# Attention stage: TensorE's work in runs of one block size, in a new order per unit

## Chip, cores and metric

The kernel runs on one core of a Trainium2 chip. The metric is the device time of one execution in microseconds; the time before is the median of three runs.

## Reference

Three layers follow each other. The change touches the first alone.

```python
def _attn_ref(q, k, v):                      # q, k, v: (4, 8, 576, 64)
    ...
    q_d, k_d, v_d = means of 4 neighbouring rows            # 144 rows
    out_up = np.repeat(sm_attn(q_d, k_d, v_d), 4, axis=2)   # full softmax attention of the pooled rows
    mask = np.abs(pos[:, None] - pos[None, :]) < 4
    scores = np.where(mask, scale * q @ k.T, -1e9)          # a band of 7 keys per query
    out_local = softmax(scores) @ v
    return out_up + out_local
...
x = attn_out.transpose(0, 2, 1, 3).reshape(B * S, H * D)    # (2304, 512)
x = _moe_ref(x, phi, w1, w2)     # soft mixture: logits = x @ phi, 8 experts with 4 slots each
return _moe2_ref(x, w_gate, w_noise, noise, w1, w2)         # top-2 mixture of 8 experts
```

The setup multiplies q, k and w_noise by 8 after drawing them.

## The kernel before

The attention runs over 16 units, a unit being one batch and two heads, whose two 64-wide heads fill the 128 partitions. A step loop `for p in range(-1, NU - 1)` (L586) goes through the list `SEQ` (L19) once per step and issues each named step for the unit `p - off`, where `off` stands in the table `BL` (L550); the last units are issued from the list `TSEQ` (L21). Each engine works through its own instructions in the order of these lists, so `SEQ` sets the order on every engine and on SP's queue of transfers. No scheduler changes it.

The steps of a unit u, in the order of their data:

- `ld` (L181, two steps ahead): keys and queries of the unit are loaded into `ld`, four transfers on SP's queue in rows of 64 floats; two buffers. `lV` (L197, one step ahead): four transfers for the values, two buffers, so unit u's can start when unit u - 2 has used its own.
- `A0`, `A1` (`a_pe`, L225, one step ahead): six transposes each, of keys and of queries. `a00` to `a111` (L235) evict them to `K` and `Q`. `KD` (L253) sums four neighbouring keys on GpSimd; `DQ0` and `DQ1` (L242) do so for the queries of one head each, `DQ0` on GpSimd in two additions, `DQ1` on VectorE in one reduce.
- `S` (`b_s`, L283): the band's scores in PSUM, a bf16 matmul that writes the mask (L285), then 20 matmuls of 35 columns (L289). `SD` (L294): pooled scores (L300). `M`, `EL`, `EX`, `SU`, `P0`, `P1` are the band's softmax, the last two on GpSimd (L333); `MD`, `DX`, `RD`, `DM` are the pooled one, of which `DM` (L362), the division by the sum, runs on GpSimd in place.
- one step later: `CP` and `CD` (L370, L380) transpose the two attention matrices; `EP00` to `EP11`, `ED0`, `ED1` evict them to `PT` and `PdT`. `VD` (L261) pools the values by matmuls, `V0`, `V1` evict them to `Vd`. `DP` (L405) and `DD` (L417) multiply by the values, `DD` with 128 and then 16 rows. `x0`, `x1`, `XA` evict and add.
- two steps later: `EP` (L437) transposes the unit's output, `X0`, `X1` keep it, `LG` (L459) computes the slot logits with four matmuls of 128 columns into 32 partitions each and a fifth into all 128, `LA` adds them up. Every fourth step also has the slots' softmax and sums (`SE`, `SS`, `ST`, `SU_`, `SK`).

All transposes and `LG` write to a ring of four PSUM buffers (`tp`, L176), so each waits until the one four before it has been evicted. `W` (L602) issues one megabyte of the soft mixture's weights per step (two in the first), of which eight matrices of two megabytes are loaded during the attention, three more when the attention's memory is free (`R2`), and the other five as buffers are released by the soft mixture's matmuls (L795, L817). `cp` (L217) puts an eviction on VectorE if its name is in `ON_V`, else on ScalarE.

## Time and profile before

| | us |
|---|---|
| median of three runs | 496.54 (495.12 to 497.39) |
| the profiled execution | 494.55 |
| its span, first to last instruction | 492.7 |
| TensorE busy | 470.2 (95%) |
| VectorE, ScalarE, GpSimd busy | 277.4, 263.4, 199.2 |

The attention's first scores start at 7 us and those of the last unit at 141 us; the soft mixture runs to about 200 us, the top-2 mixture to the end. Instructions are named by their line. A matmul in f32 stands in the trace as two records. In a list by time, the start of a block of TensorE less the start of the one before is the time that the block took, since matmuls overlap in the pipeline and their durations add up to more.

### The profile page before, as it was taken

How to read it: one execution, taken by the hardware profiler on the slowest of the kernel's cores; microseconds unless marked ns; L12 is line 12 of the kernel's file. 1: busy time of each engine (PE TensorE's matmuls, PEld its weight loads, DVE VectorE, ACT ScalarE, POOL GpSimd, SP SyncE). 2: the span in 40 equal slices, each digit the busy share in tenths (PEclk: the TensorE clock that was granted, in tenths of full speed). 3: DMA queues.
4: the chain of work that ended last, by engine and by line, in shares of the span. 5: the costliest groups of instructions: out<-in, count | busy, mean ns of one | idle time of the engine just before them, and what ended most of it. 6: DMA issues, size and time to landing. Idle time of an engine off the chain costs nothing.

```text
span 492.7 us, 12033 instructions
## 1 busy us (share of the span) xinstructions
PE 470.2 (95%) x4569; PEld 355.9 (72%) x4569; DVE 277.4 (56%) x720; ACT 263.4 (53%) x698; POOL 199.2 (40%) x289
## 2 busy tenths in 40 slices
PE   5999999899998999899999999999999999999993
PEld 4688877777875543467787787887887887878882
DVE  7878877777875321696579545273462544624300
ACT  2567766666775021486365465483664746727410
POOL 5565636536540100166566677422222221222222
PEclk9999999999999799999999999999999999999997
DMA  9999998989979599999988744699958856333333
GB/s 160 278 243 214 233 221 192 242 216 202 265 239 345 171 393 399 389 346 338 365 258 228 224 75 76 150 363 297 275 72 229 216 128 154 43 45 43 45 43 46
DMA packets 108423, 104.16 MB, mean 211 GB/s; under 512 B 68170, under 2 KB 78090, under 8 KB 108362
## 3 DMA queue, kind: packets, MB, share of 16 engines
q1 hardware_dynamic: 101450, 90.50, 61.2%
q0 software_dynamic: 6912, 12.85, 16.6%
q8 instruction: 38, 0.62, 0.5%
q14 instruction: 23, 0.19, 0.1%
HBM read 83.60 MB, written 19.73 MB: 210 GB/s over the span
## 4 chain that ended last, share of the span: by engine, by line
PE 73%; issue 9%; DMA 7%; DVE 3%; POOL 2%; ACT 2%; POOLq 2%; SPq 0%; ACTq 0%; DVEq 0%
PE y L1054 34%; DMA wr<-in_moe_w_dram 5%; PE S L289 4%; PE t L231 3%; PE gx L871 3%; PE xl L421 3%; PE Sd L300 3%; PE xl L414 2%; PE t L375 2%; PE xl L268 2%; PE t L441 2%; PE h L1034 2%; PE t L386 2%; POOL out_dram L1073 2%; POOLq L1079 1%
## 5 line engine op out<-in xcount | busy, mean ns | idle before, releaser
L1054 PE MATMUL y<-whi,hl 128*128 128x512 f32 x320 | 127.3, 398 | 0.0
L1054 PE MATMUL y<-whi,hh 128*128 128x512 f32 x320 | 126.7, 396 | 0.4 <-ACT hh L1035 0.4
L1054 PE MATMUL y<-wlo,hh 128*128 128x512 f32 x320 | 126.5, 395 | 0.0
L1073 POOL DMA_INDIRECT out_dram<-ys,idx x40 | 64.5, 1612 | 107.9 <-ACT ys L1065 56.3
L1065 ACT ACTIVATE ys<-y,gt 128x512 f32<-128x512 f32 x40 | 27.4, 686 | 82.4 <-issue 46.9
L1026 DVE TENSOR_TENSOR wlo<-wr,whi 128x512 fp32r<-128x512 f32 x64 | 42.0, 692 | 50.3 <-ACT whi L1023 49.9
L1054 PEld LDWEIGHTS y<-wlo,hh 128*128 128x128 f32 x320 | 60.1, 188 | 12.9 <-issue 1.0
L1054 PEld LDWEIGHTS y<-whi,hl 128*128 128x128 f32 x320 | 60.1, 188 | 12.3 <-issue 2.1
L1054 PEld LDWEIGHTS y<-whi,hh 128*128 128x128 f32 x320 | 60.2, 188 | 11.8 <-ACT hh L1035 0.6
L333 POOL TENSOR_TENSOR P<-El,su 64x350 f32<-64x350 f32 x31 | 23.9, 772 | 59.7 <-DVE su L326 38.3
L1036 DVE SCALAR_TENSOR_TENSOR hl<-h,hh 128x256 fp32r<-128x256 f32 (+1 forms) x64 | 31.3, 489 | 16.0 <-ACT hh L1035 14.7
L1000 POOL DMA_INDIRECT tab<-stk,pos x36 | 35.6, 990 | 11.5 <-issue 10.7
L1036 DVE SCALAR_TENSOR_TENSOR hl<-gx,hh 128x256 fp32r<-128x256 f32 (+1 forms) x64 | 31.2, 487 | 10.7 <-ACT hh L1035 9.1
L1023 ACT ACTIVATE whi<-wr 128x512 fp32r<-128x512 f32 x64 | 36.9, 625 | 0.2
L1035 ACT ACTIVATE hh<-gx 128x256 fp32r<-128x256 f32 (+1 forms) x64 | 28.1, 439 | 15.0 <-PE gx L1034 12.5
L1035 ACT ACTIVATE hh<-h 128x256 fp32r<-128x256 f32 (+1 forms) x64 | 28.0, 437 | 12.5 <-PE h L1034 10.2
L1072 POOL MEMSET spacer<- 1x1 f32 x40 | 13.6, 340 | 41.6 <-issue 41.6
L219 ACT ACTIVATE PT<-t 64x256 f32<-64x256 f32 (+1 forms) x50 | 20.6, 417 | 13.5 <-PE t L375 12.7
L919 DVE TENSOR_TENSOR oh<-iot,R 128x256 fp32r<-128x256 f32 (+2 forms) x50 | 20.3, 439 | 11.4 <-PE xs L937 9.6
L231 PE MATMUL t<-idf,ld 96*128 96x96 f32 x192 | 21.1, 259 | 4.9 <-DMA ld<-in_k_dram 4.3
L219 ACT ACTIVATE xT<-xl 128x290 f32<-128x290 f32 x32 | 11.5, 411 | 26.2 <-PE xl L421 24.1
L289 PE MATMUL S<-K,Q 128*64 128x35 f32 x640 | 23.1, 231 | 2.2 <-issue 1.4
(301 smaller groups left out, 837.8 us busy)
## 6 DMA issues: line engine op xcount, KB each, us to landing
wr<-in_moe_w_dram SPq DMA_DIRECT2D x120, 256.0 KB, 5.6
wr<-in_moe_w_dram SPq DMA_DIRECT2D x56, 512.0 KB, 7.1
out_dram<-zero SPq DMA_DIRECT2D x20, 256.0 KB, 3.4
V<-in_v_dram SPq DMA_DIRECT2D x62, 80.0 KB, 5.2
ld<-in_k_dram SPq DMA_DIRECT2D x32, 144.0 KB, 4.7
ld<-in_q_dram SPq DMA_DIRECT2D x32, 144.0 KB, 4.4
XT<-tab SPq DMA_DIRECT2D x5, 320.0 KB, 5.6
tab<-zero SPq DMA_DIRECT2D x6, 256.0 KB, 4.8
```

The lines of the kernel that those rows point to most:

```text
L219: nc.scalar.activation(dst, src, AF.Copy)
L231: nc.tensor.transpose(t[:, 96 * c:96 * c + 96], ld[:, i, 3 * j + c].rearrange("p h d -> p (h d)"), idf[0:96, 0:96])
L289: nc.tensor.matmul(s[64 * a:64 * a + 64, KW * g:KW * g + KW], Q[:, c0:c0 + 32].rearrange("p i h -> p (i h)"), K[:, c0:c0 + KW], start=Fals ...
L333: eng.tensor_tensor(P[as_, :, HQ * a:HQ * a + KW], El[as_], su[as_, :, None].to_broadcast([64, NG, KW]), op=ALU.mult)
L1000: st = nc.gpsimd.indirect_dma_start(out=tab, out_offset=bass.IndirectOffsetOnAxis(ap=pos[:, c, i:i + 1], axis=0), in_=stk[:, i].bitcast(F3 ...
L1023: nc.scalar.activation(whi[:, kk], wb(kk), AF.Copy)
L1026: eng.tensor_tensor(wlo[:, kk], wb(kk), whi[:, kk].bitcast(F32), op=ALU.subtract)
L1035: nc.scalar.activation(hh[:, f], h, AF.Relu)
L1036: nc.vector.scalar_tensor_tensor(hl[:, f], h, 0.0, hh[:, f].bitcast(F32), op0=ALU.max, op1=ALU.subtract)
L1054: nc.tensor.matmul(y, l[:, kk, ts_], r_[:, kk], start=(m == 0), stop=(m == 23))
L1065: nc.scalar.activation(ys, YS.pop((e, ti)), AF.Copy, scale=gt[:, ti:ti + 1])
L1073: st = nc.gpsimd.indirect_dma_start(out=out, out_offset=bass.IndirectOffsetOnAxis(ap=idx[:, ti:ti + 1], axis=0), in_=ys, in_offset=None, c ...
```

## The change

- `SEQ` is put in a new order. On TensorE a step now is S, A0, A1, SD, (SK, ST), CP, VD, (SU_), LG, CD, EP, DP, DD; it was S, (SK), CP, (ST), SD, CD, A0, (SU_), A1, VD, DP, EP, LG, DD. On SP's queue it stays ld, W, lV.
- The mask matmul is split into two of 64 output partitions. LG's fifth matmul becomes four of 32 output partitions. DD multiplies with 128 rows both times; the unused rows of `Vd` and `PdT`, which get one fixed buffer each, are cleared once.
- LG writes into the PSUM buffer of the scores of unit u + 2, after their softmax has read them.
- `DQ1` runs on GpSimd in two additions like `DQ0`, except for the last unit.
- `DM` is issued one step later: behind `P0` and `P1` of its unit on GpSimd; `TSEQ` gets a `DM:14` after `S:15`.
- Five other names stand in `ON_V`. The copies of `phi` are gone.

```diff
-SEQ = """S SK CP EP01 ld EP10 M EP00 ST SD CD z EP11 ED0 EL SS MD A0 ED1 EX a00 W a01 SU SU_ A1 P1 a100 a101
-a110 a111 P0 KD DQ0 VD z DP V0 V1 DQ1 DX EP LG DD x1 LA lV x0 X1 SE RD DM X0 XA""".split()
-TSEQ = """S:15 CP:14 W EP01:14 ...
+SEQ = """S ld DM M A0 a00 a01 A1 a110 a101 a100 EL SD a111 SK ST CP MD VD EP11 SS EP01 EP00 V0 EP10 V1 SU_ KD LG LA EX CD
+DQ1 W EP DP lV ED0 DX x1 ED1 DD x0 X0 X1 DQ0 SE SU P0 RD P1 XA""".split()
+TSEQ = """S:15 DM:14 CP:14 W EP01:14 ...
-ON_V = ['a110', 'a111', 'p00', 'v0', 'v1']
+ON_V = ['p11', 'k1', 'd1', 'a100', 'v0']
...
-    phi4 = const.tile([128, 4, 4 * NS], F32, name="phi4")
+    phi = const.tile([128, 4, NS], F32, name="phi")
...
+        PdT = a2.tile([128, 2, 2, 144], F32, name="PdT")
+        Vd = a2.tile([128, 2, 128], F32, name="Vd")
...
         def a_dve(u, h):
             hs = slice(64 * h, 64 * h + 64)
-            if h:
+            if h and u == NU - 1:
                 return nc.vector.tensor_reduce(out=Dq[hs, :, h], ...
...
-            nc.tensor.matmul(s[:, 0:NG * KW], idb, mask.rearrange("p g k -> p (g k)"), start=True, stop=True)
+            for a in range(2):
+                as_ = slice(64 * a, 64 * a + 64)
+                nc.tensor.matmul(s[as_, 0:NG * KW], idb[:, as_], mask.rearrange("p g k -> p (g k)"), start=True, stop=True,
+                                 skip_group_check=True)
...
-            SS[u] = s
+            SS[u] = SB[u] = s
...
-            xl, PdT, Vd = XL[u], CT[u, 1][0], VQ.pop(u)[1]
-            for kb, n in enumerate((128, 16)):
+            xl = XL[u]
+            for kb in range(2):
                 for h in range(2):
-                    nc.tensor.matmul(xl[64 * h:64 * h + 64, 1, 290:434], Vd[0:n, kb, 64 * h:64 * h + 64], PdT[0:n, kb, h],
+                    nc.tensor.matmul(xl[64 * h:64 * h + 64, 1, 290:434], Vd[:, kb, 64 * h:64 * h + 64], PdT[:, kb, h],
                                      start=(kb == 0), stop=(kb == 1), skip_group_check=True)
...
-            L = (ET_[u][1] if t2 is None else t2)[:, 128:320]
+            L = SB[u + 2][:, 0:192] if not TAIL else ET_[u][1][:, 128:320] if u in ET_ else tp()[:, 0:192]
             for t in range(4):
-                nc.tensor.matmul(L[32 * t:32 * t + 32, 0:128], phi4[:, kk, 0:NS], xT[:, 128 * t:128 * t + 128],
+                nc.tensor.matmul(L[32 * t:32 * t + 32, 0:128], phi[:, kk], xT[:, 128 * t:128 * t + 128],
                                  start=True, stop=True, skip_group_check=True)
-            nc.tensor.matmul(L[:, 128:192], phi4[:, kk], xT[:, 512:576], start=True, stop=True, skip_group_check=True)
+            for t in range(4):
+                nc.tensor.matmul(L[32 * t:32 * t + 32, 128:192], phi[:, kk], xT[:, 512:576], start=True, stop=True,
+                                 skip_group_check=True)
...
-              "DX": (soft_d2, 0, ()), "RD": (soft_d3, 0, ()), "DM": (soft_dm, 0, ()), "CP": (c_p, 1, ()),
+              "DX": (soft_d2, 0, ()), "RD": (soft_d3, 0, ()), "DM": (soft_dm, 1, ()), "CP": (c_p, 1, ()),
...
                 if p == -1 and nm == "lV":
                     nc.gpsimd.memset(PT, 0.0)
+                    nc.gpsimd.memset(Vd[:, 1], 0.0)
+                    nc.gpsimd.memset(PdT[:, 1], 0.0)
```

## Rows read from the trace of the kernel before

**Rows 1.** Stages: us, busy us of PE PEld DVE ACT POOL, PEclk, DMA share, GB/s
```profile
24.40:131.07 106.67, 105.27 (x1878) 83.90 (x1876) 83.98 (x221) 72.88 (x251) 58.36 (x86) 1.00 0.95 223
170.00:195.00 25.00, 25.00 (x314) 10.40 (x312) 5.51 (x17) 4.96 (x9) 1.58 (x5) 1.00 1.03 387
```
**Rows 2.** Chain of waits in order of time: start us, us, what
```profile
170.05 5.40 DMA wr<-in_moe_w_dram
...
190.83 6.00 DMA wr<-in_moe_w_dram
```

**Rows 3.** TensorE by time, one unit: start us, us, line, tiles, shapes, records
```profile
41.36 0.32 PE L285 MATMUL S<-mask,idb 128*128 128x350 bf16 x1
...
42.90 0.77 PE L375 MATMUL t<-idf,P 128*128 128x128 f32 x5
43.51 0.90 PE L300 MATMUL Sd<-kd,Dq 128*96 128x144 f32 x6
44.24 0.66 PE L386 MATMUL t<-idf,Ed 96*128 96x96 f32 x6
44.89 1.21 PE L231 MATMUL t<-idf,ld 96*128 96x96 f32 x12
...
46.81 0.81 PE L414 MATMUL xl<-PT,V 64*64 64x58 f32 x40
47.55 0.66 PE L441 MATMUL t<-idf,xT 128*128 128x128 f32 x4
48.04 0.27 PE L443 MATMUL t<-idf,xT 128*64 128x128 f32 x1
...
48.60 0.43 PE L465 MATMUL t<-xT,phi 128*128 128x64 f32 x2
48.97 0.86 PE L421 MATMUL xl<-PdT,Vd 128*64 128x144 f32 x8
49.75 0.32 PE L285 MATMUL S<-mask,idb 128*128 128x350 bf16 x1
```

**Rows 4.** GpSimd's groups: L249 with min/median/max ns, L251 and L333 with busy us, mean ns
```profile
L249 POOL TENSOR_TENSOR s<-Q x16: 937/942/1002, 7.9 to 140.2; 64x288 f32<-64x288 f32 x16
...
L251 POOL TENSOR_TENSOR Dq<-s 64x144 f32<-64x144 f32 x12 | 5.0, 420 | 0.9
...
L333 POOL TENSOR_TENSOR P<-El,su 64x350 f32<-64x350 f32 x31 | 23.9, 772 | 59.7 <-DVE su L326 38.3
```

**Rows 5.** SP's queue by time: start us, us of issuing, line, transfer, how many
```profile
39.98 3.23 SPq L207 DMA_DIRECT2D V<-in_v_dram  x4
43.26 3.49 SPq L186 DMA_DIRECT2D ld<-in_k_dram  x2
46.79 1.99 SPq L186 DMA_DIRECT2D ld<-in_q_dram  x2
48.84 1.16 SPq L101 DMA_DIRECT2D wr<-in_moe_w_dram  x2
50.10 2.66 SPq L207 DMA_DIRECT2D V<-in_v_dram  x4
...
127.85 2.02 SPq L186 DMA_DIRECT2D ld<-in_q_dram  x2
```

**Rows 6.** Waits of SP's queue, 16.6 to 126.4 us: us in total, times, longest
```profile
SPq L207 <- PE S L289: 2.9, 6, 0.7
...
SPq L207 <- PE xl L421: 0.3, 1, 0.3
```

**Rows 7.** Transfers into `ld` issued from 127.8 to 129.9 us
```profile
DMA to landing us min/median/max: 4.9/4.9/4.9
```

**Rows 8.** TensorE by time at the last full unit's end, columns as in Rows 3
```profile
135.56 1.06 PE L519 MATMUL t<-xK,Et 128*32 128x512 f32 x8
...
136.91 0.71 PE L231 MATMUL t<-idf,ld 96*128 96x96 f32 x6
...
141.28 0.32 PE L285 MATMUL S<-mask,idb 128*128 128x350 bf16 x1
```

More of the change, by code (lines that the diff above doesn't have):

```diff
@@ L17 @@
 CAP = 640
-SEQ = """S SK CP EP01 ld EP10 M EP00 ST SD CD z EP11 ED0 EL SS MD A0 ED1 EX a00 W a01 SU SU_ A1 P1 a100 a101
-a110 a111 P0 KD DQ0 VD z DP V0 V1 DQ1 DX EP LG DD x1 LA lV x0 X1 SE RD DM X0 XA""".split()
-TSEQ = """S:15 CP:14 W EP01:14 EP00:14 SD:15 M:15 EL:15 EP10:14 EX:15 EP11:14 CD:14 ED0:14 MD:15 SU:15 VD:14 DP:14 V0:14 V1:14 EP:13
+SEQ = """S ld DM M A0 a00 a01 A1 a110 a101 a100 EL SD a111 SK ST CP MD VD EP11 SS EP01 EP00 V0 EP10 V1 SU_ KD LG LA EX CD
+DQ1 W EP DP lV ED0 DX x1 ED1 DD x0 X0 X1 DQ0 SE SU P0 RD P1 XA""".split()
+TSEQ = """S:15 DM:14 CP:14 W EP01:14 EP00:14 SD:15 M:15 EL:15 EP10:14 EX:15 EP11:14 CD:14 ED0:14 MD:15 SU:15 VD:14 DP:14 V0:14 V1:14 EP:13
 ED1:14 P0:15 P1:15 DD:14 DX:15 LG:13 X0:13 RD:15 x0:14 DM:15 x1:14 CP:15 LA:13 EP00:15 X1:13 EP01:15 EP11:15
@@ L177, in tp @@
             return ps.tile([128, 512], F32, name="t", bufs=4)
-        LD, VQ, KD, DQ, SD, SS, PD, PL, XL, XT, XK = ({} for _ in range(11))
+        LD, KD, DQ, SD, SS, SB, PD, PL, XL, XT, XK = ({} for _ in range(11))
         def load(u):
@@ L273, in v_pe @@
                                  skip_group_check=True)
-            VQ[u] = (None, wk.tile([128, 2, 128], F32, name="Vd", bufs=1))
         def v_evac(u, i):
-            xl, Vd = XL[u], VQ[u][1]
+            xl = XL[u]
             if i:
@@ L388, in c_d @@
                 tt.append(t)
-            PdT = wk.tile([128, 2, 2, 144], F32, name="PdT", bufs=1)
-            CT[u, 1] = (PdT, tt)
+            CT[u, 1] = tt
         def c_ep(u, i, g2):
@@ L399, in c_ed @@
         def c_ed(u, kb):
-            PdT, tt = CT[u, 1]
+            tt = CT[u, 1]
             n = (128, 16)[kb]
@@ L417, in d_d @@
         def d_d(u):
-            xl, PdT, Vd = XL[u], CT[u, 1][0], VQ.pop(u)[1]
-            for kb, n in enumerate((128, 16)):
+            xl = XL[u]
+            for kb in range(2):
                 for h in range(2):
-                    nc.tensor.matmul(xl[64 * h:64 * h + 64, 1, 290:434], Vd[0:n, kb, 64 * h:64 * h + 64], PdT[0:n, kb, h],
+                    nc.tensor.matmul(xl[64 * h:64 * h + 64, 1, 290:434], Vd[:, kb, 64 * h:64 * h + 64], PdT[:, kb, h],
                                      start=(kb == 0), stop=(kb == 1), skip_group_check=True)
@@ L444, in e_pe, with e_evac @@
             ET_[u] = (t, t2)
-            if u % 4 == 0:
+        def e_evac(u, i):
+            if u // 4 not in XK:
                 XK[u // 4] = xp.tile([128, 5, 4, 128], F32, name="xK", bufs=1)
-        def e_evac(u, i):
             t = ET_[u][i]
@@ L457, in attn_moe_moe_kernel, with logit_pe @@
         LL = {}
-        def logit_pe(u, t2=None):
+        def logit_pe(u):
             xT, kk = XT[u], u % 4
-            L = (ET_[u][1] if t2 is None else t2)[:, 128:320]
+            L = SB[u + 2][:, 0:192] if not TAIL else ET_[u][1][:, 128:320] if u in ET_ else tp()[:, 0:192]
             for t in range(4):
-                nc.tensor.matmul(L[32 * t:32 * t + 32, 0:128], phi4[:, kk, 0:NS], xT[:, 128 * t:128 * t + 128],
+                nc.tensor.matmul(L[32 * t:32 * t + 32, 0:128], phi[:, kk], xT[:, 128 * t:128 * t + 128],
                                  start=True, stop=True, skip_group_check=True)
-            nc.tensor.matmul(L[:, 128:192], phi4[:, kk], xT[:, 512:576], start=True, stop=True, skip_group_check=True)
+            for t in range(4):
+                nc.tensor.matmul(L[32 * t:32 * t + 32, 128:192], phi[:, kk], xT[:, 512:576], start=True, stop=True,
+                                 skip_group_check=True)
             LL[u] = L
@@ L587, in attn_moe_moe_kernel @@
             if p == 0:
-                nc.sync.dma_start(out=phi4[:, :, 0:NS], in_=moe_phi.rearrange("(k p) s -> p k s", p=128))
+                nc.sync.dma_start(out=phi, in_=moe_phi.rearrange("(k p) s -> p k s", p=128))
             if p >= 5 and small:
@@ L611, in attn_moe_moe_kernel @@
                 consts()
-            if p == 1:
-                nc.vector.tensor_copy(phi4[:, :, NS:4 * NS].rearrange("p k (t s) -> p k t s", t=3),
-                                      phi4[:, :, None, 0:NS].to_broadcast([128, 4, 3, NS]))
         m = ms_[(B - 1) % 2]
@@ L670, in attn_moe_moe_kernel @@
               "SI": slot_in, "UA": lambda: slot_u(B - 1, (0, 1)), "UB": lambda: slot_u(B - 1, (2, 3)),
-              "LG:15": lambda: logit_pe(NU - 1, tp()), "W": flush}
+              "W": flush}
         TAIL.append(1)
```

## Prediction

> **What bounds the kernel now.** I read the table by stage first. From 24.4 to 131.1 us, twelve units of the attention, TensorE is busy 105.27 of 106.67 us, at the granted clock 1.00; the DMA engines stand at 0.95 of their time there, and move only 223 GB/s, against 387 GB/s at 1.03 in the stage after it [rows 1]. So two resources are near full in the stretch that the change touches, and the first question is which of them sets the end once TensorE gets shorter. Then the chain of waits: after the attention it runs for 27 us through weight transfers, the first and the last of four pieces at 170.05 and 190.83 [rows 2]. These transfers start when the first expert's weights have been read, which happens after the attention. Whatever the attention's end gains is gained by everything behind it; there is no slack in between.
>
> **One unit on TensorE** [rows 3]. The rows are block starts; the unit from mask to mask takes 49.75 - 41.36 = 8.39 us without a pause. The scores of the pooled part (L300) give the price of a column: 6 records of 144 columns in 0.73 us, 0.122 us each, 0.85 ns a column (records are two per matmul, and up to four stand side by side where the output is 32 wide, two where it is 64). With that price each block has its own work, and what is left over is spent at its edges. L441: four records of 128 columns, own 0.435, take 0.49: 0.06 lost on entering. L443 and L463 behind it: own 0.109 and 2 x 0.109, together 0.56 from 48.04 to 48.60: 0.23 on leaving the one, entering and leaving the other. L465: own 2 x 0.054, takes 0.37: 0.26. L421: two waves of 144 columns twice, own 0.49, takes 0.78: 0.29 for two sizes (128 rows, then 16). Against these, L375 to L300 to L386 (all of the 128-wide size) show no loss. So a boundary between block sizes costs about 0.15 us (0.09 to 0.26), and a unit has ten.
>
> **The change, part by part.**
> *Order on TensorE.* The new order is scores, both transposes for the next unit (A0, A1), pooled scores, CP, VD, logits, CD, EP, DP, DD. The mask is halved into the size of the scores, the fifth logits matmul becomes four of the size of the others, DD reads 128 rows twice. Left are five boundaries: scores to A0, CP to VD, logits to CD, EP to DP, DP to DD. The unit's own work is A 0.98, SD 0.73, CP 0.545, CD 0.49, EP 0.545, VD 0.65, logits 0.33, DD 0.49, and for the blocks that are paced per instruction their lengths less what their boundaries cost: mask and scores 1.54 (41.36 to 42.90) less 0.20, DP 0.74 less 0.10. Sum 6.75; with five boundaries at 0.15 it is 7.5 us (7.2 to 8.05 at 0.09 and 0.26). The pause behind CD (L386 takes 0.65, own 0.49), where A0 waits for a transpose buffer, goes too: A0 now follows the scores, and its buffers were emptied behind the CD of the unit before. Halved mask and quartered logits cost nothing if they stand side by side, and 0.15 + 0.33 if they don't. So TensorE alone would fall from 8.39 to about 7.5, 0.9 us a unit.
> *Queries' sums.* VectorE loses a reduce per unit; GpSimd gains the pair that it already does for the other head, 0.94 + 0.42 [rows 4]. GpSimd is busy 58.36 us of twelve units, 4.9 each [rows 1]; with 1.4 more it has 6.3 of 7.5. The sums are needed by the next unit's SD, which stands most of a period later; cover enough, and 1.4 us if it were gone.
> *Pooled scaling one unit later (DM).* It stays on GpSimd, now behind P1 of the same unit and ahead of the next unit's KD. CD waits for it, more than 4 us into the next unit; nothing is late in the steady state. In the tail it is: TSEQ now opens with DM:14 behind P0 and P1 (0.77 each [rows 4]), and CP:14 stands 1.5 us behind the start of S:15 (41.36 to 42.90 in rows 3). SU of unit 14 now comes behind X1, that is behind EP, some 1.3 us (DP, DD, boundaries) ahead of S:15; with X1's eviction, SU and two P's after it CP:14 waits 0 to 1 us; I take 0.6.
> *Evictions moved between ScalarE and VectorE.* VectorE 83.98, ScalarE 72.88 of 106.67 [rows 1]: both have over 20% left, and each loses about as much as it gets. Costed at nothing; if VectorE's order (X1, SU, RD, XA, then the next M) turned critical, its busy time would be the bound, 83.98 / 12 = 7.0 a unit before the reduce leaves, under TensorE's 7.5.
> *The loads.* This is where I think it is decided. ld, W and lV stay in this order on SP's queue, so SP's list of transfers is the same. Does SP wait for TensorE now? One cycle of it [rows 5]: V 39.98 + 3.23 = 43.21, ld of k 43.26 + 3.49 = 46.75, ld of q 46.79 + 1.99 = 48.78, weights 48.84 + 1.16 = 50.00, and the next V at once, at 50.10. No gap is over 0.1 us; what makes it long are issues that last 1 to 3 us, where transfers are behind. The view of waits puts 28 L207 issues down to TensorE, 12.5 us on nine lines, of which the first and the last stand in [rows 6]; none is over 0.7, which is the length of one issue (3.23 for four), so no wait can be told from the issue itself. So SP runs flat out, whatever TensorE does, and ld of unit 15 comes when it comes: q issued at 127.85, the second half 1.5 later, 4.9 to its landing [rows 5, 7]: 133.4 to 134.3, say 133.7.
>
> **The sum.** In the kernel before, the second half of A for unit 15 starts at 136.91, 3.2 us behind that landing, and S:15 starts at 141.28 [rows 8]. The new order takes A 2 us into the unit instead of 3.5, so it asks for the landing earlier, and more work stands between A and the next scores. From A1 on, in the last full unit: A1 0.5, SD 0.73, the two transposes of ST 0.22, CP 0.545, VD 0.65, slot sums 1.35 with their boundaries (135.56 to 136.91 [rows 8]), logits 0.33, CD 0.49, EP 0.545, DP 0.64, DD 0.49, four boundaries 0.6: 7.1 us. S:15 starts at 133.7 + 7.1 = 140.8 at best, 0.5 us earlier. The 0.9 us a unit that TensorE saves turns into a wait of A for ld. The start-up (both kernels wait for chains of single steps there) can differ by a microsecond or two, and this is swallowed by the same wait. In the tail boundaries go as well: mask 0.1, two DDs 0.15 each, three fifth logits 0.2 each, 1.0 in all, of which I put 0.7 on the path; against it 0.6 for CP:14. Together -0.5 - 0.7 + 0.6 = -0.6 us. The profiled execution took 494.55 us (span 492.7), so 493.95 of that kind; the median of the three runs, 496.54, is 1.99 above it, so I forecast 495.9, with 493.5 to 498 for this case alone (the landing's 0.9, the tail's 0 to 1.0 either way, and the unknown 0.5 of halves not side by side, twice).
>
> **The rivals.**
> 1. *TensorE sets the pace.* The boundary cost is in the rows, and each unit sheds five. The Trainium skill, TensorEngine Tiling (Array Packing), section Tiling Modes, says that a change of tiling mode drains the engine; by that rule the trace agrees, and by it alone this would be the forecast. Thirteen units from S:2 to S:15 at 0.9 are 11.7, with the tail's 0.6 it is 482.3, 484.2 as a median. Against it: ld can't land so early unless the transfers run faster than they do flat out. Chance 0.10.
> 2. *Part of the stream's time is a wait for TensorE.* If the 12.5 us of [rows 6] are real waits, and half of them is given back, the landing moves 5 to 6 us: 488.5 as profiled, 490.5 as a median. Against it: each of them is as long as one issue and no longer. Chance 0.10.
> 3. *Slower: the loads begin to wait for DP.* lV of a unit needs the V buffer, free when DP of two units before is done. In the new order DP stands 4.8 us behind A1's start, and A1 behind ld. The loop V issues, ld issues, landing, A1 to DP takes 3.23 + 5.5 + 4 + 4.8 = 17.5 us for two units; two cycles of the stream like the one shown take 2 x 10.12. So 2.7 us are spare here, in shorter cycles less; I take 1 us. Should the stretch from A1 to DP last longer than its blocks by more than that (evictions, GpSimd's sums or Vd late), SP waits, the next ld is late, A is late, and DP again. One microsecond over that point costs half a microsecond a unit, 12 x 0.5 = 6: 500 as profiled, 502 as a median. A way into it: the Trainium skill, SBUF — State Buffer, section Who interferes with whom, says that GpSimd and some two-input VectorE instructions lock each other out for a whole instruction, which speaks against more sums on GpSimd; here L249 took 937 to 1002 ns in all 16 units [rows 4], whatever VectorE did, so I give it little. Chance 0.10.
> That the halves don't stand side by side belongs to the forecast: it would make TensorE's unit 8.0, still under the stream's.
>
> **Chances and range.** Forecast 0.70, rivals 0.10 each. A measurement of this kernel tells about 0.5%, 2.5 us, from no change. Faster by more: rivals 1 and 2 and 0.05 of the forecast, 0.25; slower by more: rival 3 and 0.02 of the forecast, 0.12; within 0.5%: 0.63. The range that leaves out rival 1, half of rival 2 and most of rival 3 is 490.5 to 499.
>
> **What would show it.** Right: A's first transposes (L231) wait for ld in most units, TensorE idle about 1 us a unit, though its blocks without the waits last 7.5; boundaries gone inside S and DD; SP's issues without gaps and ld of unit 15 landing within a microsecond of 133.7; S:15 near 140.8. Wrong: a unit of 7.5 without idle time (rival 1); the last ld landing several us earlier (rival 2); gaps ahead of L207 issues ended by DP, L414 (rival 3).

## The result, and the profile after

| | before | after |
|---|---|---|
| median, runs taken side by side (us) | 495.35 (493.24 to 497.39) | 501.15 (500.24 to 501.86) |
| ratio after : before | | 1.0137, 95% interval 1.0101 to 1.0173 |
| span of the profiled execution | 492.7 | 500.1 |
| scores of the second and third unit, S:1 and S:2, start at | 14.5, 24.4 | 16.9, 26.8 |
| S:15 starts at | 141.3 | 146.4 |
| first expert's matmuls start at | 164.4 | 169.4 |
| from there to the end of the span | 328.3 | 330.7 |

The change made the kernel 1.4% slower, 5.8 us; 495.9 had been forecast, with 490.5 to 499 as range. (Times in us are medians of all runs; the ratios, here and below, leave out runs more than 1.5% above the fastest of their kernel.) In the profiled executions 2.4 of the 7.4 us arise before S:2, 2.7 between S:2 and S:15, nothing (-0.1) between S:15 and the first expert, 2.4 behind that.

The stage table answers to [rows 1] (columns as there). This line holds the units 2 to 13, as the line from 24.40 to 131.07 did before.

```profile
26.83:136.61 109.78, 95.47 (x1965) 83.54 (x1961) 78.15 (x210) 79.33 (x252) 74.93 (x108) 1.00 0.93 217
```

TensorE, which had paused for 1.4 us in that stretch, now pauses for 14.3; it does its work in 95.5 us instead of 105.3, and the stretch is 3.1 us longer all the same. The DMA engines are less busy, 0.93 against 0.95. So it is neither TensorE's work nor the transfers that end last. The view of waits of the same kernel from 24.4 to 131 us (who waited for whom: us in total, times, longest) names who does:

```profile
DVE Q L223 <- ACT Q L221: 14.4, 12, 1.2
PE xl L424 <- ACT xT L221: 13.2, 12, 1.2
...
ACT PT L221 <- DVE PT L223: 7.6, 11, 1.2
```

One wait of TensorE's makes up nearly all of its pause: DD (L424) waits for ScalarE's eviction `x1` in every unit, 12 times, 13.2 us. One unit on TensorE, in order of time (start us, us, line, and in brackets how long the engine was idle before and who ended it), answers to [rows 3]:

```profile
45.34 0.32 PE L288 MATMUL S<-mask,idb 128*64 128x350 bf16 x2
45.48 1.31 PE L293 MATMUL S<-K,Q 128*64 128x35 f32 x40
46.73 1.21 PE L233 MATMUL t<-idf,ld 96*128 96x96 f32 x12
...
51.69 0.81 PE L417 MATMUL xl<-PT,V 64*64 64x58 f32 x40
53.71 0.71 PE L424 MATMUL xl<-PdT,Vd 128*64 128x144 f32 x8 [1.21 <-ACT xT L221]
54.25 0.32 PE L288 MATMUL S<-mask,idb 128*64 128x350 bf16 x2
```

The unit takes 54.25 - 45.34 = 8.91 us, against 8.39 before. DP starts at 51.69, and 2.02 us pass until DD starts; without a wait DP took 0.74 [rows 3]. What held `x1` up stands in the same stretch of VectorE, ScalarE and GpSimd (one line is one instruction or a run of the same):

```profile
48.03 1.34 ACT L221 ACTIVATE Q<-t 64x288 f32<-64x288 f32 x3
49.27 0.97 ACT L221 ACTIVATE PT<-t 64x384 f32<-64x384 f32 x2
51.03 0.38 ACT L221 ACTIVATE PT<-t 64x256 f32<-64x256 f32 x1 [0.80 <-DVE PT L223]
...
53.27 0.39 ACT L221 ACTIVATE xT<-xl 128x290 f32<-128x290 f32 x1
```
```profile
48.56 0.45 DVE L223 COPY Q<-t 64x288 f32<-64x288 f32 x1 [1.19 <-ACT Q L221]
48.93 0.50 DVE L318 TENSOR_TENSOR El<-S,m 128x350 f32<-128x350 f32 x1
49.36 0.59 DVE L343 TENSOR_REDUCE md<-Sd 96x3 f32<-96x432 f32 x1
49.99 0.49 DVE L346 TENSOR_SCALAR nmd<-md 96x3 f32<-96x3 f32 x1
50.51 0.43 DVE L223 COPY PT<-t 64x256 f32<-64x256 f32 x1
```
```profile
49.51 0.94 POOL L251 TENSOR_TENSOR s<-Q 64x288 f32<-64x288 f32 x1 [0.27 <-ACT Q L221]
50.54 0.42 POOL L253 TENSOR_TENSOR Dq<-s 64x144 f32<-64x144 f32 x1
```

Read in order of time it is one loop through all engines. Scores, then A (46.73). ScalarE evicts `a110` from A's buffer (48.03); VectorE has been idle for 1.19 us for it, since its `a100` reads the same buffer and stands next in its queue. Behind `a100` (48.56) come EL, MD's reduce and `nmd`, a scaling of 96x3 numbers. `nmd` starts at 49.99 and ends at 50.48, just when GpSimd's addition of the queries' sums ends (49.51 + 0.94 = 50.45). Behind `nmd` is `EP11` (50.51), and ScalarE's `EP10`, which reads the same buffer as `EP11`, has waited for it for 0.80 us (51.03). Behind that on ScalarE stand V1, EX, ED0 and DX's six instructions; then `x1` at 53.27. DD follows, behind it the next scores, and the next A. In the kernel before, `x1` stood behind DD, and nothing of this ended on TensorE.

### The profile page after: what moved, and what is told of

Same layout as the page of the kernel before. It is cut to its first block, busy times and chain, and to the rows that moved or that the text cites. A ratio compares the mean times of both kernels' runs of the same rounds, so it can differ in the third digit from the quotient of the medians.

```text
span 500.1 us, 12283 instructions
## 1 busy us (share of the span) xinstructions
PE 464.1 (93%) x4681; PEld 359.8 (72%) x4681; DVE 269.6 (54%) x702; ACT 272.2 (54%) x700; POOL 220.0 (44%) x321
## 4 chain that ended last, share of the span: by engine, by line
PE 61%; issue 11%; ACT 9%; DVE 7%; DMA 6%; POOL 3%; POOLq 2%; SPq 1%; ACTq 0%; DVEq 0%
PE y L1058 34%; DMA wr<-in_moe_w_dram 3%; PE hp L799 3%; ACT Ed L355 3%; PE S L293 3%; PE gx L875 2%; PE xl L424 2%; PE t L233 2%; PE yacc L821 2%; PE h L1038 2%; POOL out_dram L1077 2%; POOLq L1083 1%; PE gx L1038 1%; PE Sd L304 1%; ACT xT L221 1%
## 5 line engine op out<-in xcount | busy, mean ns | idle before, releaser
L1077 POOL DMA_INDIRECT out_dram<-ys,idx x40 | 63.8, 1595 | 113.4 <-ACT ys L1069 56.9
L1058 PEld LDWEIGHTS y<-whi,hl 128*128 128x128 f32 x320 | 60.6, 189 | 11.4 <-issue 2.1
L1039 ACT ACTIVATE hh<-gx 128x256 fp32r<-128x256 f32 (+1 forms) x64 | 28.1, 439 | 15.9 <-PE gx L1038 12.9
L1039 ACT ACTIVATE hh<-h 128x256 fp32r<-128x256 f32 (+1 forms) x64 | 27.9, 436 | 13.5 <-PE h L1038 9.8
L251 POOL TENSOR_TENSOR s<-Q 64x288 f32<-64x288 f32 x31 | 29.3, 944 | 6.3 <-ACT Q L221 3.0
L221 ACT ACTIVATE PT<-t 64x384 f32<-64x384 f32 (+1 forms) x50 | 21.9, 442 | 12.2 <-DVE PT L223 8.4
L424 PE MATMUL xl<-PdT,Vd 128*64 128x144 f32 x128 | 11.4, 298 | 15.8 <-ACT xT L221 15.1
```

The source lines that it names most:

```text
L221: nc.scalar.activation(dst, src, AF.Copy)
L251: nc.gpsimd.tensor_tensor(q2, q4[:, :, 0:2], q4[:, :, 2:4], op=ALU.add)
L1039: nc.scalar.activation(hh[:, f], h, AF.Relu)
L1058: nc.tensor.matmul(y, l[:, kk, ts_], r_[:, kk], start=(m == 0), stop=(m == 23))
L1077: st = nc.gpsimd.indirect_dma_start(out=out, out_offset=bass.IndirectOffsetOnAxis(ap=idx[:, ti:ti + 1], axis=0), in_=ys, in_offset=None, c ...
```

## The experiments

The units are those between steps without slot work; "S:2 to S:15" and S:15 are starts of TensorE's mask blocks in the profiled execution. The ratio is against the kernel before, run on the same chip alongside; it rests on ten runs each, four for the fewer edges and for the sums alone. S:2 and S:15 come from one execution of each, which lies up to 3.4 us from the median of its runs. So the units, which repeat to about 0.01 us within a trace, are firmer than a difference of a few us in S:15.

| run | ratio (95%) | unit | S:2 | S:2 to S:15 | S:15 |
|---|---|---|---|---|---|
| before | 1 | 8.39 | 24.4 | 116.9 | 141.3 |
| after | 1.0137 (1.0101, 1.0173) | 8.91 | 26.8 | 119.6 | 146.4 |
| x1 behind DD | 1.0015 (0.9965, 1.0064) | 7.66 and more | 25.1 | 116.6 | 141.7 |
| EL early | 1.0038 (0.9990, 1.0086) | 8.09 | 26.5 | 116.0 | 142.5 |
| both | 1.0011 (0.9974, 1.0049) | mixed | 25.4 | 116.8 | 142.1 |
| sums on VectorE | 1.0024 (0.9983, 1.0065) | 8.74 | 25.6 | 117.5 | 143.0 |
| nmd on ScalarE | 1.0019 (0.9982, 1.0056) | 8.39 | 24.6 | 118.2 | 142.8 |
| EP11 on ScalarE | 1.0018 (0.9971, 1.0064) | 8.34 | 26.7 | 114.6 | 141.4 |
| a100 on ScalarE | 1.0010 (0.9979, 1.0042) | 8.26 | 27.9 | 114.2 | 142.1 |
| evictions back | 0.9993 (0.9952, 1.0033) | 8.08 | 27.1 | 113.4 | 140.6 |
| old order, even blocks | 0.9936 (0.9892, 0.9980) | 8.06 | 24.1 | 112.6 | 136.7 |
| the same, early Vd | 0.9935 (0.9891, 0.9979) | 8.15 | 24.9 | 113.0 | 137.8 |

### Where DD's wait comes from

**x1 behind DD.** Only the direction of one dependency turns; no engine's order changes.

```diff
-DQ1 W EP DP lV ED0 DX x1 ED1 DD x0 X0 X1 DQ0 SE SU P0 RD P1 XA""".split()
+DQ1 W EP DP lV ED0 DX ED1 DD x1 x0 X0 X1 DQ0 SE SU P0 RD P1 XA""".split()
```

> The changed kernel with one step exchanged: the eviction x1 is issued behind DD instead of ahead of it. The order of instructions on every engine is the same as in the changed kernel; only the dependency on the PSUM tile xl turns round: x1 waits for DD, DD no longer for x1. Theory (DD's wait for x1 is what lengthens the unit): TensorE's unit falls from 8.91 us by the 1.3 that it waits there, to about 7.6; thirteen units give 13 to 16 us, so about 487. Rival A (the loads' stream is the next bound, as the forecast had it): A waits for ld instead, the unit stops at 8.3 to 8.4, about 495. Rival B (the wait only moves to another step of the same loop through ScalarE and VectorE): unit 8.8 or more, about 500.

Measured: 494.16 us, the wait gone, and in its place what the forecast had put there. Waits of TensorE from 24.4 to 131 us, and two of its units:

```profile
PE t L233 <- DMA ld<-in_q_dram: 5.6, 6, 2.2
```
```profile
41.05 0.32 PE L288 MATMUL S<-mask,idb 128*64 128x350 bf16 x2
...
49.06 0.32 PE L288 MATMUL S<-mask,idb 128*64 128x350 bf16 x2
51.84 0.69 PE L233 MATMUL t<-idf,ld 96*128 96x96 f32 x6 [0.49 <-DMA ld<-in_k_dram]
53.37 0.69 PE L233 MATMUL t<-idf,ld 96*128 96x96 f32 x6 [0.84 <-DMA ld<-in_q_dram]
...
60.47 0.32 PE L288 MATMUL S<-mask,idb 128*64 128x350 bf16 x2
```

Some units are 7.66 long (the one that ends at 41.05 here; the run without weights, below, has 7.67, and both edits together, next but one, have single units of 7.40), then one takes 11.4, with A waiting for ld twice. These waits are 1.33 us; most of the rest is TensorE itself, which is busy 9.49 us there instead of 7.58. Its granted clock shows why. Two units of this run, the 11.4 and one of 12.65 us (columns as in [rows 1]):

```profile
49.06:60.47 11.41, 9.49 (x165) 8.35 (x161) 7.05 (x17) 6.80 (x23) 6.28 (x9) 0.85 1.01 227
111.96:124.61 12.65, 10.41 (x165) 9.29 (x161) 6.95 (x18) 6.93 (x23) 6.23 (x9) 0.73 1.04 240
```

In each it stood at 0.50, the lower of its two levels (1.2 of 2.4 GHz), for some 3 and 6 us, behind a pause of TensorE. So the theory names the cause of the loss, and rival A says how far it can be repaired in this run: S:15 at 141.7, where the forecast had 140.8. That the two lie so close is luck in part: from the busy times, some 4.7 us of it are the lower clock in these two units (an estimate: 9.49 and 10.41 less 7.6 each), which neither the theory nor the forecast had. Without them S:15 would stand at about 137, near the 136.7 of the old order with even blocks.

**EL early**, still with x1 ahead of DD: on VectorE, EL no longer stands behind `a100`.

```diff
-SEQ = """S ld DM M A0 a00 a01 A1 a110 a101 a100 EL SD a111 SK ST CP MD VD EP11 ...
+SEQ = """S ld DM M A0 a00 a01 EL A1 a110 a101 a100 SD a111 SK ST CP MD VD EP11 ...
```

> The changed kernel with one step moved on VectorE: EL stands ahead of the eviction a100, which waits 1.2 us for ScalarE's a110 on the same PSUM buffer. x1 stays ahead of DD. Theory (one loop: a110, a100, EL, MD, EP11, EP10, EX, DX, x1, DD, scores, transposes): everything from MD to x1 comes 0.4 to 0.5 us earlier, the unit is 8.4 to 8.5, about 495. Rival (DD waits for x1 because of ScalarE's own queue, not because of VectorE): unit 8.9, 501.

Measured: 495.94 us, unit 8.09: 0.82 less, more than the 0.4 to 0.5 of the theory; the median of `nmd`, which EL's early place also moves, is back at 166 ns there. **Both edits together:**

> The changed kernel with both edits: x1 behind DD, EL ahead of a100. Theory: as with x1 behind DD alone or up to 0.2 us a unit shorter, since DD no longer ends the loop and EL has slack: 484 to 487. Rival A (loads): 495, as with the first edit alone. Rival B: if another wait of the loop binds after the first edit, this one gives a further 0.3 to 0.4 a unit, 4 to 5 us.

494.31 us; A waits for the queries' ld in eight units. Nothing is added: rival A.

**The queries' sums back on VectorE** in all units:

```diff
-            if h and u == NU - 1:
+            if h:
```

> The changed kernel with the queries' sums back on VectorE for both kinds of unit (the reduce per unit that the change took away). The forecast has them covered either way, and DD's wait for x1 stays what it is: 500 to 502, unit 8.9. Rival (the sums on GpSimd or the lock between GpSimd and VectorE are part of the loss): over 2 us faster, 498 or less. Rival (VectorE is in the loop, and the reduce of 0.6 us stands in it): 0.3 to 0.6 a unit slower, 505 to 509.

My theory fell: 494.79 us, not 500 to 502. The rows of `nmd` (min/median/max ns, first and last start us) of the kernel before, of after, of this run, and of the run with a100 on ScalarE, in this order:

```profile
L342 DVE TENSOR_SCALAR nmd<-md x16: 165/165/167, 13.1 to 145.0; 96x3 f32<-96x3 f32 x16
```
```profile
L346 DVE TENSOR_SCALAR nmd<-md x16: 165/502/940, 15.8 to 150.3; 96x3 f32<-96x3 f32 x16
```
```profile
L346 DVE TENSOR_SCALAR nmd<-md x16: 165/310/941, 14.7 to 147.2; 96x3 f32<-96x3 f32 x16
```
```profile
L346 DVE TENSOR_SCALAR nmd<-md x16: 165/166/942, 15.9 to 146.1; 96x3 f32<-96x3 f32 x16
```

An instruction of 165 ns takes three times as long in the changed kernel. With one head's sums fewer on GpSimd it meets the end of the addition that is left, and the unit is 8.91 - 8.74 = 0.17 us shorter; the median of `nmd` falls by 0.19. Another 1.2 us lie at the start: S:2 at 25.6 instead of 26.8 (see the part on the start-up). **nmd on ScalarE** takes the same instruction out of GpSimd's way and leaves the sums where they are:

```diff
-            nc.vector.tensor_scalar(nmd, md, -1.0 / 128, None, op0=ALU.mult)
...
+        def soft_nm(u):
+            nc.scalar.activation(PD[u], MDS.pop(u), AF.Copy, scale=-1.0 / 128)
```

> The changed kernel with one small instruction moved: the scaling of the pooled maxima (nmd, 96x3) goes from VectorE to ScalarE, behind EP00; x1 stays ahead of DD, the sums stay on GpSimd. On VectorE it took 502 ns in the median (165 in the kernel before), and ended each time with GpSimd's addition of the queries' sums. Theory (that hold-up stands in the loop that ends in DD's wait for x1): EP11 and all behind it 0.3 to 0.5 us earlier, unit 8.5 to 8.6 instead of 8.91, about 497. Rival (the loop runs through ScalarE's own queue and gets nothing from it): unit 8.9, 501.

494.34 us, unit 8.39 (78.28 to 86.66 us): the hold-up cost 0.5 us a unit. S:2 stands at 24.6, but the move of `nmd` did not bring that: SD and the filler matmuls ahead of S:1, which took 1.55 and 1.97 us in the changed kernel, take 0.81 and 1.08 here, and in a later run that has `nmd` on ScalarE as well (with x1 behind DD) they take 1.55 and 1.97 again, with S:1 at 16.9. What differs is how long TensorE works at half its later speed after the start (more in the part on the start-up).

**The evictions.** First the old list:

```diff
-ON_V = ['p11', 'k1', 'd1', 'a100', 'v0']
+ON_V = ['a110', 'a111', 'p00', 'v0', 'v1']
```

> The changed kernel with the list of evictions on VectorE of the kernel before (a110, a111, p00, v0, v1); order, sums and x1 as in the changed kernel. The forecast had the move at nothing. Theory (the loop runs through GpSimd's hold-up of nmd and ScalarE's DX ahead of x1, and any split leaves these two): unit 8.7 to 9.1, 499 to 503. Rival (the pairs of evictions from one buffer on two engines, a110 and a100, EP11 and EP10, are what lengthens it): unit 8.5 or less, under 497.

The rival held: unit 8.08, 493.35 us. Then one name each off VectorE's new list, `p11` and `a100`:

> The changed kernel with the eviction EP11 on ScalarE (as in the kernel before) instead of VectorE; all else as changed. Theory (the pair EP11, EP10: ScalarE's queue waits 0.8 us for VectorE, whose EP11 stands behind nmd): ScalarE does EP11 itself in 0.38 while VectorE is held up, EX, DX and x1 come 0.4 us earlier, unit 8.4 to 8.5, 495 to 497. Rival (the pair a110, a100): unit 8.9, 501.

> The changed kernel with the eviction a100 on ScalarE (as in the kernel before) instead of VectorE; all else as changed. Theory (the pair EP11, EP10 sets the loop): VectorE's EL and MD are earlier, but ScalarE has 0.43 us more ahead of EP01, EP00 and EP10, so x1 is not earlier: unit 8.8 to 9.0, 500 to 502. Rival (the pair a110, a100 sets the loop through EL and MD): unit 8.4 to 8.6, 495 to 497.

```profile
43.77 0.32 PE L288 MATMUL S<-mask,idb 128*64 128x350 bf16 x2
...
51.57 0.71 PE L424 MATMUL xl<-PdT,Vd 128*64 128x144 f32 x8 [0.88 <-ACT xT L221]
52.11 0.32 PE L288 MATMUL S<-mask,idb 128*64 128x350 bf16 x2
```
```profile
44.40 0.32 PE L288 MATMUL S<-mask,idb 128*64 128x350 bf16 x2
...
52.11 0.71 PE L424 MATMUL xl<-PdT,Vd 128*64 128x144 f32 x8 [0.79 <-ACT xT L221]
52.66 0.32 PE L288 MATMUL S<-mask,idb 128*64 128x350 bf16 x2
```

EP11 on ScalarE (first fence): 493.12 us, unit 8.34. a100 on ScalarE (second): 493.77 us, unit 8.26. The second theory fell: I had held that only one of the pairs sets the loop, and that `a100` would not matter. Both stand in it, one behind the other; `a100` early lets EL, MD and `nmd` start earlier, `nmd` ahead of GpSimd's addition (the last of the four `nmd` rows: 166 ns). So there is one loop, and every step taken out of it shortens the unit by what it held: 0.17 (one head's sums), 0.52 (`nmd`), 0.57 (EP11), 0.65 (a100), 0.82 (EL), 0.83 (all evictions), 1.25 (x1, which opens it).

**Evictions and sums back** together (the two diffs above):

> The changed kernel with the old list of evictions and the queries' sums back on VectorE: of the change are left TensorE's new order and edits and the pooled scaling a unit later. Theory (the sums still cost the start-up 1.5 us; after it the transfers' pace holds, 112.6 to 113.4 from S:2 to S:15): S:2 at 25.5, S:15 at 138.5 to 139, 491 to 493. Rival (VectorE, with the reduce back, gets too slow for the unit of 8.08): unit 8.3 or more, 495.

496.00 us, ratio 0.9996 (0.9952 to 1.0041): no more than either edit. In the profiled execution S:2 is at 26.5 and S:15 at 143.4, both later than the theory had them. Around S:2 TensorE's clock is at the lower level, from 25.4 to 31.9 us: the unit from 26.49 to 37.15 takes 10.66 us, against 8.75 for the same unit with the evictions alone back.

### What stands behind it: the transfers

**No weights in the loop**, x1 behind DD:

```diff
-NW = [2] + [1] * 14
+NW = [0] * 15
```

> The changed kernel with x1 behind DD, and no soft-mixture weights loaded during the attention's loop: all 16 MB are issued at its end. The end of the kernel gets later for that, so what counts is the start of S:15, 141.7 us with x1 behind DD alone, where A's transposes wait for ld in six units. Theory (the weights' bytes ahead of ld keep it late): no wait for ld, TensorE's unit is its own blocks, 7.5 to 7.7, S:15 at 128 to 132. Rival (ld is late because it is issued behind lV, which waits for DP of the step before): the wait stays, S:15 at 138 to 142.

```profile
49.08 0.32 PE L288 MATMUL S<-mask,idb 128*64 128x350 bf16 x2
...
56.75 0.32 PE L288 MATMUL S<-mask,idb 128*64 128x350 bf16 x2
```
```profile
24.40:131.00 106.60, 104.29 (x2170) 91.22 (x2165) 84.58 (x229) 86.80 (x284) 81.17 (x117) 1.00 0.53 111
```

The theory held, in one run. A unit is 56.75 - 49.08 = 7.67 us, without a wait for ld, TensorE is busy 104.3 of 106.6 us, the DMA engines 0.53 of their time, and S:15 starts at 131.9. (The end, 521.7 us, pays for the late weights.) So the new order is worth 0.72 us a unit on TensorE, and with the weights in the loop their bytes keep it from that.

**ld a unit earlier**, x1 behind DD:

```diff
-        load(0)
+        load(0), load(1)
...
-        BL = {"ld": (load, -2, ()), ...
+        BL = {"ld": (load, -3, ()), ...
```

and in the order ld stands between DQ1 and W instead of behind S.

> The changed kernel with x1 behind DD, and ld issued a whole unit earlier: behind A1 of the step before, as soon as its buffer is free; the weights and lV keep their places behind it. Theory (ld is late by its place in the queue): no wait for ld; the DMA engines' own work, 0.98 of 8.06 to 8.4 us a unit, sets the pace at 8.0 to 8.1, S:15 at 136 to 137.5, 489 to 490. Rival (the DMA engines have no more to give in this order): S:15 at 141 as with x1 behind DD alone, 494.

```profile
24.40:131.00 106.60, 97.08 (x2037) 86.13 (x2028) 79.00 (x217) 82.04 (x267) 79.21 (x114) 1.00 1.01 231
```

Half right: A no longer waits, S:2 to S:15 falls to 113.0 us and S:15 to 138.2, with the DMA engines at 1.01 of their time; now VD waits for V (5.6 us in four units). But the median is 494.57, ratio 1.0034. Why S:15 comes 3 us earlier than in the kernel before and the end does not, stays open; what goes with it is the clock, whose mean over the execution is 0.981 in these ten runs and 0.990 in those of the kernel before beside them (last section). Two variants of it, the sums on VectorE as well, and then the last two megabytes of weights behind the loop:

> The changed kernel with x1 behind DD, ld a unit earlier, and the queries' sums back on VectorE. Theory (with the first two the transfers set the pace, S:2 to S:15 in 113.0 us as in the old order with even blocks, 112.6): the sums give back only the start-up's 1 to 2 us, S:15 at 136.5 to 137.5, 491 to 493. Rival (the hold-up of VectorE's small instructions is part of that pace): S:2 to S:15 in under 111 us, S:15 at 135 or earlier, under 490.

> As the run with x1 behind DD, ld ahead and the sums back, and the last two megabytes of weights are issued after the attention's loop instead of in its last two steps. Theory (transfers set the pace in the loop, and DMA engines stand idle some 3 us after it, where SP waits for buffers): S:15 3 to 5.4 us earlier (two megabytes at the 387 GB/s of the stage behind are 5.4), at 132 to 134; of that 0 to 3 us is left at the end, 488 to 491. Rival (the weights are awaited behind the attention, so that all of it comes back): S:15 earlier, the end as in the run without this edit.

494.95 us (1.0006, 0.9961 to 1.0050) and 494.91 us (1.0032, 0.9993 to 1.0072). The first missed its theory: S:2 to S:15 took 120.6 us, since the last full unit alone took 15.1; TensorE stood 3.3 us in the middle of its scores there, waiting for nothing that the trace shows, and its clock fell to the lower level behind that (0.77 over the unit). The second brought S:15 from 144.1 to 140.0, and all of it was gone at the end: the weights are awaited behind the attention, its rival. **nmd on ScalarE and x1 behind DD** together:

> The changed kernel with both repairs: nmd on ScalarE and x1 behind DD. Theory (either repair alone ends at the transfers' pace): as either alone, S:2 to S:15 115 to 118 us, A's transposes waiting for ld in several units, 492 to 495. Rival (the repairs add up): units of 7.6 to 8.0 throughout, S:2 to S:15 under 112, under 490.

497.14 us, 1.0071 (1.0029 to 1.0112): the repairs don't add up, they are even worse than either. A waits for ld 7.1 us in eight waits, and three units take 11.0, 11.8 and 14.2 us. That the transfers set the pace is shown by the run without weights. What the three long units have beyond their waits is the clock, at 0.85, 0.86 and 0.76: TensorE is busy 9.22, 9.17 and 12.04 us in them, against 7.4 to 7.6 in its other units, and 9.3 in the last full unit of the run with x1 behind DD, at 1.00: some 6 us together. Without these S:2 to S:15 would be about 113 us (an estimate), as in the runs that are bound by the transfers and keep the clock.

### The change's parts in the old order

**Even blocks.** The kernel before, its order, evictions, sums and pooled scaling; of the change only TensorE's three edits (and the fixed, once cleared `Vd` and `PdT`, and logits in the scores' buffer, which they need):

```diff
+            for a in range(2):
+                as_ = slice(64 * a, 64 * a + 64)
+                nc.tensor.matmul(s[as_, 0:NG * KW], idb[:, as_], ...
...
+            for kb in range(2):
...
+            for t in range(4):
+                nc.tensor.matmul(L[32 * t:32 * t + 32, 128:192], ...
```

> The kernel before in its own order of steps, its own split of the evictions, the queries' sums on VectorE and the pooled scaling where it was; only TensorE's three edits are made: mask in two halves, logits' fifth matmul in four quarters, DD with 128 rows twice. They take 0.10 to 0.15 (DD 0.78 to 0.54 gives 0.24, logits 0.2, mask 0.1) each, some 0.5 us, out of TensorE's unit of 8.39. The forecast's theory (the loads' stream runs flat out whatever TensorE does): no change, 494 to 496, with A waiting about 0.5 us a unit for ld. Rival (TensorE sets the pace): 13 x 0.5 = 6.5 less, 489.

```profile
24.40:131.00 106.60, 103.67 (x2025) 88.09 (x2020) 87.35 (x230) 77.08 (x266) 60.77 (x89) 1.00 0.99 232
```

489.10 us, 0.64% faster than the kernel before. The unit is 8.06, A waits for no ld, and the DMA engines are at 0.99: SP's stream has become faster with TensorE. The rival held. (The profiled execution is the fastest of the ten.)

**Fewer edges**: the same, with logits ahead of VD and EP ahead of DP.

```diff
-... P0 KD DQ0 VD z DP V0 V1 DQ1 DX EP LG DD x1 LA lV ...
+... P0 KD DQ0 LG VD EP DP V0 V1 DQ1 DX DD x1 LA lV ...
```

> The kernel before in its own order with TensorE's three edits (as in the run with the old order and even blocks: 489.1, unit 8.06), and on TensorE logits moved ahead of VD and EP ahead of DP, so that two boundaries between block sizes go. Theory (a boundary costs 0.15 and TensorE sets the pace): unit 7.75, S:15 at 132.5 to 134, 485. Rival (the DMA engines, at 0.98 to 0.99 of their time there, are the floor): unit 8.0, no change against that run, 488 to 490, with A waiting for ld.

497.24 us, 1.0104 (1.0030 to 1.0179), unit 8.95: neither. Two boundaries fewer made it 8 us slower, by waits that the edit itself made (TensorE's waits, 24.4 to 131 us):

```profile
PE xl L424 <- DVE Vd L223: 7.2, 11, 0.7
PE S L288 <- DVE LT L479: 3.5, 8, 0.4
```

With V0, V1 and LA right behind VD on their engines (`LG VD V0 V1 LA EP DP DQ1 DX DD x1 lV`) these are gone:

> The kernel before in its own order with TensorE's three edits and two boundaries fewer (logits ahead of VD, EP ahead of DP), as in the slower trial, but Vd's evictions and the logits' sum now stand right behind VD on their engines instead of behind DP and x1. Theory (that trial's unit of 8.95 came from DD waiting for Vd and the next mask for the logits' sum): both waits gone, unit 7.7 to 8.0, S:2 to S:15 between 108 and 112, 486 to 489. Rival (the transfers' pace, 112.6 from S:2 to S:15, is the floor): as with the old order and even blocks, 488 to 490.

490.17 us, 0.9935, unit 8.15, with DP now waiting 3.1 us in seven units for Vd's eviction, and the DMA engines at 1.01. Its rival: like the even blocks alone. Both are the versions that beat the two kernels.

**The sums alone**: the kernel before with DQ1 on GpSimd.

> The kernel before with one part of the change alone: the queries' sums of the second half on GpSimd as well (two additions, the last unit excepted). The forecast put it at nothing. Theory now: the start-up pays 1 to 2 us (the sums stand behind GpSimd's clearing of PT there), and a small instruction of VectorE is held up where it meets an addition; TensorE sets the pace at 8.39 and covers that: 494.5 to 496. Rival (the hold-up reaches TensorE's path in this order too): 0.2 to 0.4 a unit, 497 to 500.

511.75 us, 1.0354 (1.0268 to 1.0441); neither theory came near. TensorE and GpSimd in one unit:

```profile
46.28 0.32 PE L285 MATMUL S<-mask,idb 128*128 128x350 bf16 x1
...
49.52 0.98 PE L300 MATMUL Sd<-kd,Dq 128*96 128x144 f32 x6 [0.93 <-POOL Dq L251]
...
55.93 0.32 PE L285 MATMUL S<-mask,idb 128*128 128x350 bf16 x1
```
```profile
46.50 0.94 POOL L249 TENSOR_TENSOR s<-Q 64x288 f32<-64x288 f32 x1
47.52 0.42 POOL L251 TENSOR_TENSOR Dq<-s 64x144 f32<-64x144 f32 x1
48.02 0.94 POOL L249 TENSOR_TENSOR s<-Q 64x288 f32<-64x288 f32 x1
49.04 0.42 POOL L251 TENSOR_TENSOR Dq<-s 64x144 f32<-64x144 f32 x1
49.54 0.90 POOL L365 TENSOR_TENSOR Ed<-Ed,rd 96x432 f32<-96x432 f32 x1
```

In the old order P0, P1 and KD stand ahead of the sums, SD waits for the second of them, and the pooled scaling that CD's transposes need stands behind both. `nmd` stays at 165 ns. GpSimd has the time, but not at that place. Some of the 17.5 us (roughly 5, from three units of 11.6 to 12.9 us at a clock of 0.85 to 0.87) comes by the clock that falls behind such waits.

## Why the prediction was wrong, point by point

**TensorE's boundaries: right.** 7.5 us a unit was forecast (7.2 to 8.05); the run without weights shows 7.67, and single units of the run with both edits 7.40. Ends of blocks at 0.15 us could be read from the rows before.

**Evictions "costed at nothing": the step that failed.** I compared VectorE's and ScalarE's busy time with the unit and found both 20% below it. That answers whether an engine can do its work in a period, not whether its results come in time. The change makes TensorE wait for `x1`, and puts `x1` behind DX, DX behind MD, MD behind `a100`, `a100` behind A: a chain that begins and ends on TensorE in one unit. Read off the changed kernel's rows, from scores to scores, it is 8.9 us, with none of VectorE, ScalarE and GpSimd busy over 73% of the time. I had listed the order of steps and never followed `x1`; its waits could be read only afterwards, but the chain itself stood in the new list. The old list of evictions alone takes 0.83 us out of it.

**Queries' sums "cover enough": right for SD, wrong for VectorE.** In the new order SD never waits for them in the steady state. But they hold up `nmd`: 165 ns became 502. The prediction named a rule on two-input instructions of VectorE (`nmd` has one input), and read it in one direction: it looked at L249, GpSimd's instruction, which kept its length [rows 4], and let the matter go. The rows show VectorE's small instruction held until GpSimd's ends. The Trainium skill, SBUF — State Buffer, section Who interferes with whom, says as much: a `tensor_scalar` can run in a mode that takes the ports shared with GpSimd, and of two instructions that want them the one that comes second is blocked for the whole length of the first. By that rule the trace agrees, to 0.03 us (50.48 against 50.45). "Cover" also belongs to a place: in the old order the same sums cost 3.5%.

**The loads "decide": right as the second bound, mis-sized, and not the first.** In the changed kernel TensorE waits for `x1`, not for ld. Once `x1` is out of the way A does wait for ld, and S:15 is at 141.7 (forecast 140.8, partly by luck, as said above). But "SP runs flat out, whatever TensorE does" was wrong as a price. In the old order with even blocks the same stream, with the same bytes, is 4.3 us faster from S:2 to S:15 (112.6 against 116.9). I had taken 0.95 of the DMA engines' time as full; the same loads reach 0.99 to 1.01. So part of that time was a wait for TensorE, as rival 2 had it, though the view of waits can't size it (in the faster run it still puts 14.8 us of SP's down to TensorE). 6 us was rival 2's gain; TensorE's three edits by themselves give 3.2 by the ratio, 4.5 by the medians (489.1 against 493.6 side by side). Two readings were off as well. The view has 27 such issues, not 28. And the landing: by its own terms the second half of A has both heads at 127.85 + 1.5 + 4.9 = 134.3, not 133.7, which puts S:15 at 141.4, no gain.

**Rival 3** had the right size, 502, and half of the mechanism. The stretch from A1 to DP's end did become longer than its blocks, and lV does wait for DP, which it did not before [rows 6]:

```profile
SPq L209 <- PE xl L417: 11.1, 9, 2.7
```

(waits of SP's queue, 24.4 to 131 us.) But A never waits for ld in the steady state; DD pays directly, without the 1 us that I had as spare.

**Start-up**: 2.4 us, which I had said would be "swallowed by the same wait" for ld. There was no such wait to swallow it. All of it arises before S:1 (14.5 before, 16.9 after; from S:1 to S:2 both take 9.9). The first unit's SD waits 0.67 us for the sums, which stand behind GpSimd's clearing of `PT`, `Vd` and `PdT`. Nearly all the rest is speed: after the start TensorE's blocks take about twice their later time, in both kernels. In the kernel before this is over when A comes, which takes 1.18 us ahead of S:1; in the changed kernel it lasts until S:1, with 2.0 us for A, 1.55 for SD, and 1.97 instead of 1.08 for four filler matmuls. That it is the lower clock is likely, but the clock's column reads 1.00 there, so it is not shown. `nmd` takes 940 ns there as well, but only from 15.78 us on, and no block ahead of S:1 waits for it. With one head's sums on VectorE, S:1 comes 7.8 to 8.3 us after S:0, in the other runs of the new order mostly 9.5 to 9.7; what ends the slow stretch was not settled.

**The tail: right.** From S:15 to the first step of the last softmax (L637 and L633) it takes 15.27 us before, 14.38 in the old order with even blocks and 14.74 after: the boundaries give 0.89 (forecast 0.7 of 1.0), and 0.36 of that is taken back (forecast 0 to 1, 0.6 taken), with a pause of 0.30 us where CP:14 waits for GpSimd's `P`. With the old evictions, and the pooled scaling still a unit later, it is 14.38 again: it costs only when `P` is late.

**Behind the attention** 2.4 us were added that no step spoke of, of which 1.6 lie in the first 48 matmuls of the first expert (5.29 us instead of 3.69, at half of the clock; last section).

## What to carry to other kernels

Busy shares and block lengths bound an engine's throughput; before an order is changed, follow one result round the loop as well, through every queue that it stands in (here scores, transposes, an eviction on each engine, a softmax, an eviction, scores), and compare that sum with the period. Two evictions of one buffer on two engines, and a small instruction behind a long one of the engine that it shares ports with, belong into that sum with their waits. A pause of the bounding engine can also cost more than its length, where its clock falls behind it: 1.6 to 2.8 us in single units here. And an edit that takes work off the bounding engine is best tried alone first: here three edits of the change gave 0.6% without its new order, and the order, with the evictions and sums that came with it, took away more than it gave.
